# Other addresses for some operands of the matrix products in a two-layer MoE kernel

## The chip, the core and the metric

The kernel runs on one core of a Trainium2 chip. The metric is the time of one execution on the device in microseconds; a lower number is better. Three runs of the kernel before took 1744.85, 1748.18 and 1754.96 us, median 1748.18.

## What is computed

Attention with pooled keys and values (batch 8, 8 heads, 576 positions, 64 per head), then two feed-forward layers on the 4608 tokens of 512 features:

```python
# attention: keys and values averaged over 8 positions
x = attn_out.transpose(0, 2, 1, 3).reshape(B * S, H * D)
# first layer, d_ff = 2048
h = x @ w_in
g = h * np.clip(h + 3.0, 0.0, 6.0) / 6.0
x = g @ w_out
# second layer, d_ff = 1536
g = x @ w_gate
silu = g / (1.0 + np.exp(-g))
out = (silu * (x @ w_val)) @ w_out
```

## The kernel before

All products are done in a 4-byte type in three passes: each operand is split into a high part, rounded to the type, and the low rest (`split`: a copy on ACT and a subtraction on DVE), and high x high, high x low and low x high are summed in PSUM. So products come in threes.

The program has these stages, one after the other on PE:

- Attention, woven into the first up-product `up` (L623): 512 columns of tokens stream past 128x128 weights; in groups of 12 products for one tile of 128 hidden features. The last block of tokens has no attention left beside it: 204 products in a row.
- `down_b` (L891), the down-product of the first layer, for 9 blocks of 512 tokens (`NB`). It uses Strassen's scheme in Winograd's form: 7 products of quarter matrices in place of 8. Each of the 7 (`n`, listed in `DN`) walks through 4 chunks (`NCB`) of hidden features, and a chunk is 12 products of 256 columns. The stationary operand is the weights, `pw`, one tile for each of the 7; the moving operand is the chunk `gb`, split just before. 9 x 7 x 4 x 12 = 3024 products.
- For each of 6 groups of 768 tokens (`NG`): `up2` with 504 products of 384 columns (12 weight blocks, each 7 x 6 products; stationary `wr` from a ring of four buffers, moving `xc`, the split token quarters), then `down2` with 378 products of 256 columns (7 x 3 chunks x 18; stationary `gc`, the split chunk, moving `wr`). Both are issued on L712 (`mm3x`).

The order on each engine is the order in which the code is written; pools decide when a buffer is free again. Weights for `pw` come by `load_pw` from SP's queue, half a tile (1 MB) for each DMA.

What matters here is where operands lie in a partition of SBUF. In this text the **distance** of a product is the address of its moving operand less that of its stationary operand, in bytes, modulo 256. In the built program before it is 0 for all 1728 products of L623, 64 for all 3024 of `down_b`, 0 for all 3024 of `up2` and 64 for all 2268 of `down2`. Tiles with `+ 64` elements of room and a start at element 8 (`ring_tile`, `x_step`) serve to set it. In the attention, the products of L601 to L604 (256 columns at most) have their moving operand 32 above the stationary one.

In `x_step`, `what` names the quarter or sum of quarters: `11`, `T1`, `T2`, `21`, `T4`, `T3`, `22`; the seven products of a block use them in the order P1 (11), P6 (T2), P5 (T1), P2 (21), P4 (T4), P7 (T3), P3 (22). In `split_gc`, `n` counts the seven products of `down2` and `c` their three chunks.

Of the kernel before, what the change touches and what calls it, by code (L numbers as in the profile page):

```python
# [9 lines left out]
F32R = mybir.dt.float32r  # L10
# [8 lines left out]
def f32(ap):  # L19
    return ap.bitcast(F32)  # L20
# [3 lines left out]
def kernel(  # L24
# [27 lines left out]
    nc = tc.nc  # L52
    P = 128
# [31 lines left out]
    half = const.tile([P, 1], F32, name="half")  # L85
    gap_p.tile([P, 16], F32, name="gap")

    BIG = 4096
# [11 lines left out]
    M = 384  # L100
# [5 lines left out]
    NP1 = F1 // 2  # L106
    g_d = [dram.tile([P, 2, 2, NP1, MB], F32, name=f"g{j}") for j in range(NB)]
    s_w1 = dram.tile([P, 7, NP1, 2, 2 * P], F32, name="sw1")
# [90 lines left out]
    B7 = {"11": 0, "T1": 1, "21": 2, "T2": 3, "22": 4, "T3": 5, "T4": 6, "12": 7}  # L199
# [441 lines left out]
    def store_g(j, f, g):  # L641
# [8 lines left out]
    DN = [("P1", "11", "11"), ("P4", "22", "T4"), ("P2", "12", "21"), ("P6", "S2", "T2"),  # L650
          ("P5", "S1", "T1"), ("P7", "S3", "T3"), ("P3", "S4", "22")]
    HALF = 4
    CH = 2
    l2 = {}
    xc, ys, gf, gc, wr = {}, {}, {}, {}, {}

    def load_y(p):
# [5 lines left out]
            nc.sync.dma_start(out=t[:, 2 * r + c], in_=y_d[:, 2 * r:2 * r + 2, t0:t0 + M])  # L663
        ys[p] = t

    def x_step(p, n, lo_eng, sum_eng):

        t = ys[p]
        place = {"11": 0, "T1": 0, "12": 1, "T3": 1, "21": 2, "T4": 2, "22": 3, "T2": 3}
        v = lambda what: t[:, place[what]]  # L670
        what, then = [("11", "T1"), ("22", "T3"), ("T1", "T2"), ("T2", None), ("21", "T4"), ("T4", None), ("T3", None)][n]
        if what == "11":
            x = new_q7("xc")
        else:
            pool = l2["xa" if what in ("T1", "22") else "xt" if what == "T3" else "xb"]
            x = pool.tile([P, 4 * M + 64], F32R, tag="x" + what, name="xc")
        x = xc[p, what] = x[:, 8:8 + 4 * M].rearrange("p (a k n) -> p a k n", a=2, k=2)
        split(x[:, 0], x[:, 1], v(what), lo_eng)
        if then:
            sums_b(sum_eng, v, (then,))  # L680
# [87 lines left out]
    def split_gc(p, n, c, lo_eng):  # L768

        what = DN[n][1]  # L770
        t = gc[p, n, c] = l2["gc"].tile([P, 2, CH, M], F32R, tag="gc", name="gc")
        split(t[:, 0], t[:, 1], gf[p][:, GP[what], CH * c:CH * (c + 1)], lo_eng)

    def sums_g(p, ops, a, b):
# [65 lines left out]
    CB = 2  # L840
# [4 lines left out]
    def load_g(j, slot):  # L845

        if j < NB:
            r, c = divmod(slot, 2)
            t = gq[j, slot] = lb["gq"].tile([P, NP1, MB], F32, tag=f"gq{slot}", name="gq")
            nc.sync.dma_start(out=t, in_=g_d[j][:, r, c])  # L850

    def new_pw(n, t):
        lb["pw", DN[n][2]] = t.rearrange("p (f a n) -> p f a n", f=NP1, a=2)

    def load_pw(n, half):
        what, fs = DN[n][2], slice(NP1 // 2 * half, NP1 // 2 * (half + 1))
        nc.sync.dma_start(
            out=f32(lb["pw", what][:, fs]).rearrange("p f a n -> p (f a n)"),
            in_=s_w1[:, B7[what], fs].rearrange("p f a n -> p (f a n)"),
        )  # L860

    SLOT = {"11": 0, "S1": 0, "12": 1, "S4": 1, "21": 2, "S3": 2, "22": 3, "S2": 3}

# [14 lines left out]
    def down_b(i):  # L878

        j, n = divmod(i, 7)  # L880
        what = DN[n][0]
        place = "P1" if what in ("P6", "P7") else what
        if what == place:
            bb[what] = bank().rearrange("p (d n) -> p d n", d=2)
        ps, w = bb[place], lb["pw", DN[n][2]]
        for c in range(NCB):
            g = gb.pop((i, c))
            for d in range(2):
                for k in range(CB):
                    for m, (wh, gh) in enumerate(((0, 0), (0, 1), (1, 0))):  # L890
                        nc.tensor.matmul(  # L891
                            out=ps[:, d], lhsT=w[:, CB * c + k, wh, P * d:P * (d + 1)], rhs=g[:, gh, k],
                            start=what == place and (c, d, k, m) == (0, 0, 0, 0),
                            stop=(c, k, m) == (NCB - 1, CB - 1, 2), skip_group_check=True,
                        )
# [249 lines left out]
    with tc.manual_schedule():  # L1145
# [64 lines left out]
        for j in range(NB):  # L1210
            for f in range(F1):
                if (j, f) == (NB - 1, 0):
                    attn_ctx.close()
                    for nm in ("px", "gq"):
                        lb[nm] = right_b.enter_context(
                            tc.tile_pool(name=nm, bufs=1, side="right", reuse_waits="tile"))
                    new_pw(0, lb["px"].tile([P, BIG + 8], F32R, tag="px", name="pw")[:, :BIG])
                    new_pw(1, big_x("pw"))
                hp = ps_h.tile([P, N], F32, tag="h", name="h")
                up(hp, wu[f], x_tile(j))  # L1220
                attn_slot(j, 2 * f)
                gate()
                attn_slot(j, 2 * f + 1)
                gated.append((j, f, act1(hp), hp))
                if j == 0:
                    weights.convert()
                else:
                    prep_slot(F1 * (j - 1) + f)
                if j == NB - 1:
                    if f % 4 == 3:  # L1230
                        new_pw(2 + f // 4, big_w("pw"))
                    if f in first_loads:
                        kind, *args = first_loads[f]
                        (load_g if kind == "g" else load_pw)(*args)
                    if f >= F1 - NCB:
                        split_b(0, f - F1 + NCB)
# [106 lines left out]
```

## Time and profile before

| | us |
|---|---|
| median of three runs | 1748.18 |
| the profiled execution | 1749.84 |
| its span, first to last instruction | 1747.8 |
| PE busy in it | 1696.1 |
| DVE busy | 1335.7 |
| ACT busy | 751.9 |
| POOL busy | 640.9 |

The profiled execution is the one from which all rows below come; its span and 2 us around it make up its time. Busy time of PE counts products that overlap only once: a product lasts longer than the distance between the starts of two, since they are pipelined. In the timeline, products of one line that follow each other without a pause are one row, with the first start, the time from there to the last end, and their number.

### The profile page before, as it was taken

The numbers are of one execution on the slowest core, as the hardware profiler recorded it, in microseconds if no ns is written. First come the engines' busy times: TensorE is split into PE (matmuls) and PEld (weight loads), VectorE is DVE, ScalarE is ACT, GpSimd is POOL, SyncE is SP. The second block draws the span as 40 slices with busy tenths as digits, with TensorE's granted clock in tenths as the row PEclk, the third lists the DMA queues.
The fourth block names the chain that finished last, engine by engine and source line by source line (L and its number), as shares of the span: only waits on it lengthen the run. The fifth ranks groups of instructions, "written<-read, shape, count | busy, mean of one in ns | idle before, by whom it ended". The sixth has DMA issues, their size and how long they took to land.

```text
span 1747.8 us, 30757 instructions
## 1 busy us (share of the span) xinstructions
PE 1696.1 (97%) x11116; PEld 1603.2 (92%) x11116; DVE 1335.7 (76%) x2356; ACT 751.9 (43%) x1656; POOL 640.9 (37%) x821
## 2 busy tenths in 40 slices
PE   5889999999999999999999999999999999999999
PEld 4678887878788899999999999999999999999999
DVE  6888898788976678888888668668668668668665
ACT  6665554555544445555554233223224224224222
POOL 6565775766821000000000550550550550560560
PEclk8899999999999999999999999999999999999999
DMA  7766898888767965555555878878878878878776
GB/s 184 180 181 186 244 278 261 238 260 255 227 228 279 415 256 190 194 204 215 212 182 188 289 240 290 296 241 288 295 243 289 293 242 289 297 241 287 265 241 217
DMA packets 237784, 432.48 MB, mean 247 GB/s; under 512 B 87104, under 2 KB 169024, under 8 KB 220480
## 3 DMA queue, kind: packets, MB, share of 16 engines
q1 hardware_dynamic: 236576, 430.25, 74.7%
q8 instruction: 88, 1.44, 0.3%
q14 instruction: 64, 0.52, 0.1%
q10 hardware_dynamic: 1056, 0.26, 0.1%
HBM read 326.11 MB, written 104.33 MB: 246 GB/s over the span
## 4 chain that ended last, share of the span: by engine, by line
PE 86%; DVE 6%; DMA 4%; ACT 2%; issue 1%; POOL 1%; SPq 0%; DVEq 0%; POOLq 0%; ACTq 0%
PE b L712 45%; PE b L891 20%; PE h L623 17%; PE pss L503 1%; DMA q_in<-in_q_dram 1%; DVE g L638 1%; DMA wstg<-in_moe_w_in_dram 1%; PE pst L573 1%; PE pst L577 1%; PE psv L601 0%; DVE vtl L469 0%; DVE mx L513 0%; DVE qT L485 0%; PE psv L602 0%; PE psv L604 0%
## 5 line engine op out<-in xcount | busy, mean ns | idle before, releaser
L712 PE MATMUL b<-xc,wr 128*128 128x384 f32 x3024 | 527.3, 335 | 3.0 <-ACT xc L149 2.4
L712 PEld LDWEIGHTS b<-xc,wr 128*128 128x128 f32 x3024 | 525.5, 188 | 3.6 <-ACT xc L149 2.8
L623 PE MATMUL h<-x,wu 128*128 128x512 f32 x1728 | 430.0, 400 | 5.3 <-DVE g L638 5.2
L759 POOL TENSOR_TENSOR s<-s,c 128x384 f32<-128x384 f32 x144 | 142.5, 1016 | 754.3 <-ACT s L757 754.3
L721 DVE TENSOR_TENSOR c<-c,b 128x384 f32<-128x384 f32 x504 | 265.0, 552 | 175.1 <-PE b L712 151.3
L623 PEld LDWEIGHTS h<-x,wu 128*128 128x128 f32 x1728 | 320.1, 191 | 70.9 <-DVE g L638 6.7
L891 PE MATMUL b<-gb,pw 128*128 128x256 f32 x3024 | 356.8, 279 | 0.7 <-ACT gb L149 0.7
L891 PEld LDWEIGHTS b<-gb,pw 128*128 128x128 f32 x3024 | 356.4, 188 | 1.1 <-ACT gb L149 0.9
L712 PE MATMUL b<-wr,gc 128*128 128x256 f32 x2268 | 268.1, 279 | 0.0
L712 PEld LDWEIGHTS b<-wr,gc 128*128 128x128 f32 x2268 | 267.9, 188 | 0.0
L149 ACT CAST gb<-gq 128x512 fp32r<-128x512 f32 x252 | 155.0, 621 | 158.4 <-PE b L891 133.6
L150 DVE TENSOR_TENSOR gb<-gq,gb 128x512 fp32r<-128x512 f32 x252 | 167.6, 689 | 53.9 <-ACT gb L149 53.2
L766 POOL TENSOR_TENSOR gf<-s,c 128x384 f32<-128x384 f32 x144 | 168.4, 1195 | 66.6 <-DVE c L721 64.3
L149 ACT CAST gc<-gf 128x768 fp32r<-128x768 f32 x126 | 105.6, 838 | 189.0 <-POOL gf L766 101.0
L757 ACT ACTIVATE s<-c 128x384 f32<-128x384 f32 x144 | 73.4, 526 | 198.2 <-DVE c L721 197.0
L150 DVE TENSOR_TENSOR gc<-gf,gc 128x768 fp32r<-128x768 f32 x126 | 134.2, 1094 | 18.0 <-ACT gc L149 16.3
L634 ACT ACTIVATE g<-h,half 128x512 f32<-128x512 f32 x144 | 98.9, 687 | 75.7 <-PE h L623 61.4
L638 DVE SCALAR_TENSOR_TENSOR g<-g,h 128x512 f32<-128x512 f32 x144 | 97.4, 677 | 22.7 <-ACT g L634 22.5
L551 POOL TENSOR_TENSOR e<-e,sm 128x288 f32<-128x288 f32 (+4 forms) x74 | 48.3, 653 | 123.1 <-DVE sm L547 87.4
L729 ACT COPY c<-b 128x384 f32<-128x384 f32 x72 | 34.0, 472 | 128.5 <-PE b L712 128.5
L869 DVE TENSOR_TENSOR gq<-gq 128x1024 f32<-128x1024 f32 x72 | 87.8, 1219 | 0.0
L207 DVE TENSOR_TENSOR gf<-gf 128x768 f32<-128x768 f32 (+1 forms) x66 | 66.9, 1029 | 12.1 <-POOL gf L766 10.9
(101 smaller groups left out, 1657.4 us busy)
## 6 DMA issues: line engine op xcount, KB each, us to landing
wr<-sup SPq DMA_DIRECT2D x72, 1024.0 KB
wr<-sdn SPq DMA_DIRECT2D x84, 768.0 KB
wr<-sup SPq DMA_DIRECT2D x72, 768.0 KB
g<-g SPq DMA_DIRECT2D x144, 256.0 KB
gq<-g SPq DMA_DIRECT2D x36, 1024.0 KB
wstg<-in_moe_w_out_dram SPq DMA_DIRECT2D x56, 256.0 KB
pw<-sw SPq DMA_DIRECT2D x14, 1024.0 KB
sup<-s SPq DMA_DIRECT2D x12, 1024.0 KB
```

The lines of the kernel that those rows point to most:

```text
L149: nc.scalar.copy(out=hi, in_=src)
L150: lo_engine.tensor_tensor(out=lo, in0=src, in1=f32(hi), op=ALU.subtract)
L623: nc.tensor.matmul(out=ps, lhsT=w(kt, wh), rhs=x(kt, xh), start=first and n == 0, stop=last and n == 3 * len(kts) - 1,)
L634: nc.scalar.activation(out=t, in_=ps, func=ACTF.Relu, bias=half, scale=1.0 / 6.0)
L638: nc.vector.scalar_tensor_tensor(out=t, in0=t, scalar=1.0, in1=ps, op0=ALU.min, op1=ALU.mult)
L712: nc.tensor.matmul(out=ps, lhsT=w(wh), rhs=x(xh), start=first and n == 0, stop=last and n == 2)
L721: add = lambda dst, a, b: nc.vector.tensor_tensor(out=dst, in0=a, in1=b, op=ALU.add)
L757: nc.scalar.activation(out=g[q], in_=c[q], func=ACTF.Sigmoid)
L759: nc.gpsimd.tensor_tensor(out=g[q], in0=g[q], in1=c[q], op=ALU.mult)
L766: nc.gpsimd.tensor_tensor(out=gf[p][:, GP[TURN[q]], f], in0=g[q], in1=c[q], op=ALU.mult)
L869: nc.vector.tensor_tensor(out=v(what), in0=v(a), in1=v(b), op=op)
L891: nc.tensor.matmul(out=ps[:, d], lhsT=w[:, CB * c + k, wh, P * d:P * (d + 1)], rhs=g[:, gh, k], start=what == place and (c, d, k, m) == (0 ...
```

## The change

It gives other start addresses to some operand tiles, so that part of the products have another distance. Number, order and size of the products stay, line for line (the lines move by 4 to 11).

| stage | before | after |
|---|---|---|
| `down_b` | 3024 at 64 | in each of 9 blocks: 12 at 0, 12 at 64, 12 at 96, 12 at 0 (the four chunks of n = 0), then 288 at 64 |
| `up2` | 3024 at 0 | in each of 72 weight blocks of 42: 18 at 0 (P1, P6, P5), 6 at 64 (P2), 6 at 0 (P4), 6 at 32 (P7), 6 at 0 (P3) |
| `down2` | 2268 at 64 | in each of 6 groups: 18 at 0, 144 at 64, 18 at 96, 36 at 64, 18 at 0, 144 at 64 |

In all that is 2700 + 1944 products of 256 columns at 64, 432 at 0 and 216 at 96, and of the 384-column products 2160 at 0, 432 at 64 and 432 at 32.

```diff
+    GC_AT = {(0, 0): 16, (3, 0): 56, (4, 0): 16}
+    X_AT = {'21': 24, 'T3': 16}
+
     def x_step(p, n, lo_eng, sum_eng):
...
-        x = xc[p, what] = x[:, 8:8 + 4 * M].rearrange("p (a k n) -> p a k n", a=2, k=2)
+        a = X_AT.get(what, 8)
+        x = xc[p, what] = x[:, a:a + 4 * M].rearrange("p (a k n) -> p a k n", a=2, k=2)
...
     def split_gc(p, n, c, lo_eng):

         what = DN[n][1]
-        t = gc[p, n, c] = l2["gc"].tile([P, 2, CH, M], F32R, tag="gc", name="gc")
+        a = GC_AT.get((n, c), 0)
+        t = l2["gc"].tile([P, 2 * CH * M + 64], F32R, tag="gc", name="gc")[:, a:a + 2 * CH * M]
+        t = gc[p, n, c] = t.rearrange("p (a k n) -> p a k n", a=2, k=CH)
...
+    P1_AT = (16, 1088, 2168, 3216)
+
     def new_pw(n, t):
-        lb["pw", DN[n][2]] = t.rearrange("p (f a n) -> p f a n", f=NP1, a=2)
+        k = BIG // NCB
+        at = P1_AT if n == 0 else [k * c for c in range(NCB)]
+        lb["pw", DN[n][2]] = [t[:, a:a + k].rearrange("p (f a n) -> p f a n", f=CB, a=2) for a in at]

     def load_pw(n, half):
-        what, fs = DN[n][2], slice(NP1 // 2 * half, NP1 // 2 * (half + 1))
-        nc.sync.dma_start(
-            out=f32(lb["pw", what][:, fs]).rearrange("p f a n -> p (f a n)"),
-            in_=s_w1[:, B7[what], fs].rearrange("p f a n -> p (f a n)"),
-        )
+        what = DN[n][2]
+        for c in range(NCB // 2 * half, NCB // 2 * (half + 1)):
+            nc.sync.dma_start(
+                out=f32(lb["pw", what][c]).rearrange("p f a n -> p (f a n)"),
+                in_=s_w1[:, B7[what], CB * c:CB * (c + 1)].rearrange("p f a n -> p (f a n)"),
+            )
...
-                            out=ps[:, d], lhsT=w[:, CB * c + k, wh, P * d:P * (d + 1)], rhs=g[:, gh, k],
+                            out=ps[:, d], lhsT=w[c][:, k, wh, P * d:P * (d + 1)], rhs=g[:, gh, k],
...
-                    new_pw(0, lb["px"].tile([P, BIG + 8], F32R, tag="px", name="pw")[:, :BIG])
+                    new_pw(0, lb["px"].tile([P, 4296], F32R, tag="px", name="pw"))
```

The only instructions that are added are DMAs of SP. This is SP's order at the last of them, at the beginning of `down_b`, before (`g` are the stores of the first layer's gated values, `pw` the weights of `down_b`, `y` its results, `gq` the gated values read back for the next block of tokens):

```order
L642 DMA g_105<-g_7257 256x1x256
L642 DMA g_105<-g_7278 256x1x256
L857 DMA pw<-sw_106 128x2048 x8
L912 DMA y<-o_7496 128x2x256
L850 DMA gq<-g_98 128x2048 x4
```

and the same place after:

```order
L642 DMA g_105<-g_7262 256x1x256
L642 DMA g_105<-g_7284 256x1x256
L868 DMA pw<-sw_106 128x1024 x16
L923 DMA y<-o_7510 128x2x256
L856 DMA gq<-g_98 128x2048 x4
```

The eight DMAs have become sixteen of half the size, in the same place. The first six loads of `pw`, which stand singly between stores of `g`, have become pairs in the same way:

```order
 L283 DMA sup_116<-s_6907 128x1536
-L857 DMA pw<-sw_106 128x2048
+L868 DMA pw<-sw_106 128x1024 x2
 L642 DMA g_105<-g_6954 256x1x256
 L123 DMA wstg<-in_moe_w_val_dram 128x2x256 x2
```

## Rows read from the trace of the kernel before

**Rows 1.** The page: span, busy time of PE and DVE, the chain that ended last.

```profile
span 1747.8 us, 30757 instructions
...
PE 1696.1 (97%) x11116; PEld 1603.2 (92%) x11116; DVE 1335.7 (76%) x2356; ACT 751.9 (43%) x1656; POOL 640.9 (37%) x821
...
PE 86%; DVE 6%; DMA 4%; ACT 2%; issue 1%; POOL 1%; SPq 0%; DVEq 0%; POOLq 0%; ACTq 0%
PE b L712 45%; PE b L891 20%; PE h L623 17%; PE pss L503 1%; DMA q_in<-in_q_dram 1%; DVE g L638 1%; DMA wstg<-in_moe_w_in_dram 1%; PE pst L573 1%; PE pst L577 1%; PE psv L601 0%; DVE vtl L469 0%; DVE mx L513 0%; DVE qT L485 0%; PE psv L602 0%; PE psv L604 0%
```

**Rows 2.** Timeline of PE, stages after the attention: start us, us, what, count, idle before.

```profile
543.78 46.44 PE L623 MATMUL h<-x,wu 128*128 128x512 f32 x204
590.07 17.34 PE L891 MATMUL b<-gb,pw 128*128 128x256 f32 x144
608.09 339.44 PE L891 MATMUL b<-gb,pw 128*128 128x256 f32 x2880 [0.68 <-ACT gb L149]
...
1039.83 44.68 PE L712 MATMUL b<-wr,gc 128*128 128x256 f32 x378
1084.35 87.53 PE L712 MATMUL b<-xc,wr 128*128 128x384 f32 x504
1171.71 44.68 PE L712 MATMUL b<-wr,gc 128*128 128x256 f32 x378
...
1611.87 87.53 PE L712 MATMUL b<-xc,wr 128*128 128x384 f32 x504
1699.23 44.68 PE L712 MATMUL b<-wr,gc 128*128 128x256 f32 x378
```

**Rows 3.** Products by line: count, duration of one in ns (min/median/max), first and last start.

```profile
L623 PE MATMUL h<-x,wu x432: 387/389/497, 479.7 to 589.8; 128*128 128x512 f32 x144
...
L712 PE MATMUL b<-xc,wr x3024: 333/334/525, 947.4 to 1699.1; 128*128 128x384 f32 x189
L712 PE MATMUL b<-wr,gc x2268: 276/279/281, 1039.8 to 1743.6; 128*128 128x256 f32 x189
```

**Rows 4.** Timeline of PE at the end of the attention, trains of L623 and single products.

```profile
514.29 2.90 PE L623 MATMUL h<-x,wu 128*128 128x512 f32 x12
...
540.06 0.28 PE L601 MATMUL psv<-aT,vst 128*128 128x256 f32 x1
540.18 0.28 PE L602 MATMUL psv<-aT,vst 128*128 128x256 f32 x1
540.30 0.28 PE L603 MATMUL psv<-aT,vst 128*128 128x256 f32 x1
540.41 0.28 PE L604 MATMUL psv<-aTt,vtl 96*128 96x256 f32 x1
540.54 2.93 PE L623 MATMUL h<-x,wu 128*128 128x512 f32 x12
543.30 0.28 PE L601 MATMUL psv<-aT,vst 128*128 128x256 f32 x1
543.43 0.28 PE L602 MATMUL psv<-aT,vst 128*128 128x256 f32 x1
543.55 0.28 PE L603 MATMUL psv<-aT,vst 128*128 128x256 f32 x1
543.66 0.28 PE L604 MATMUL psv<-aTt,vtl 96*128 96x256 f32 x1
```

**Rows 5.** The same timeline earlier, attention products of 64 columns.

```profile
479.39 0.28 PE L602 MATMUL psv<-aT,vst 128*128 128x64 f32 x1
479.50 0.28 PE L603 MATMUL psv<-aT,vst 128*128 128x64 f32 x1
479.61 0.28 PE L604 MATMUL psv<-aTt,vtl 96*128 96x64 f32 x1
```

**Rows 6.** Three stretches (`down_b`, `up2`, `down2`): busy us (count) by engine, clock, DMA.

```profile
core 0: us, PE busy (x) PEld busy (x) DVE busy (x) ACT busy (x) POOL busy (x), PEclk, DMA share, GB/s
608.00:947.00 339.00, 338.92 (x2877) 338.95 (x2878) 289.83 (x411) 176.07 (x290) 0.00 (x0) 1.00 0.58 206
1084.35:1171.71 87.36, 87.36 (x506) 87.36 (x505) 55.43 (x95) 21.35 (x41) 47.58 (x46) 1.00 0.82 280
1171.71:1216.23 44.52, 44.52 (x380) 44.52 (x379) 38.62 (x52) 20.06 (x29) 4.26 (x3) 1.00 0.81 268
```

**Rows 7.** Timeline of SP's queue at the beginning of `down_b`.

```profile
596.47 9.39 SPq L857 DMA_DIRECT2D pw<-sw  x8
609.41 0.37 SPq L912 DMA_DIRECT2D y<-o  x1
615.44 11.63 SPq L850 DMA_DIRECT2D gq<-g  x4
```

## The prediction

> **What bounds the kernel now.** I read the page first: busy shares, then the chain that ended last [rows 1]. PE is busy 97% of the span, and three lines of matrix products hold 82% of the chain: L712 45%, L891 20%, L623 17%. No wait of any size stands between them, so from the middle of the kernel on the time is the number of products times the spacing between their starts. That spacing is read from the timeline of PE, where products that follow each other without a pause are one row [rows 2]. A row lasts from the first start to the last end, so I take off one product's own length (medians of 279, 334 and 389 ns for 256, 384 and 512 columns, [rows 3]) and divide by the count less one:
>
> - L623 after the attention, 512 columns, distance 0: (46.44 - 0.389)/203 = 226.85 ns.
> - L712 in `up2`, 384 columns, distance 0: (87.53 - 0.334)/503 = 173.35 ns.
> - L891, 256 columns, distance 64: (339.44 - 0.279)/2879 = 117.81 ns.
> - L712 in `down2`, 256 columns, distance 64: (44.68 - 0.279)/377 = 117.77 ns.
>
> The granted clock is 1.00 in these stretches [rows 6], the upper level, 2.4 GHz, where one column per cycle would be 213.3, 160.0 and 106.7 ns. So each product costs more than its columns: 13.5 and 13.35 ns at distance 0, 11.1 ns at distance 64. This surplus, not waits or other engines, is what the change can touch: 11.1 ns on 5292 products of 256 columns is 59 us, 13.35 ns on 3024 of 384 columns is 40 us.
>
> The surplus isn't one fixed number. In the attention part L623 runs in trains of 12 products. A train of the same count lasts 2.90 us in one place and 2.93 in another [rows 4]: (2.93 - 0.389)/11 = 231.0 ns a product against 226.85 in the long run, 46 ns more in a train; the shorter train has 228.3. So after other products have come between, a run needs some products to settle, and until then each costs some 4 ns more. What went before matters, at least for a while.
>
> **The change part by part.** The number, order and size of products stay. Sum against the profiled execution, 1749.84 us, span 1747.8; the median of the three runs, 1748.18, lies 0.1% below it, and I add the sum to the median.
>
> 1. The long runs, 2700 products in `down_b` and 1944 in `down2` still at distance 64, now led in by 12 or 18 products of 256 columns at distance 0. Is a led-in run faster? The trace of before has this already in another shape: each of the six `down2` stretches follows 504 products at distance 0, and `down_b` follows 204 of them. All six `down2` rows read 44.68 us [rows 2], and the run of L891 that starts afresh after an idle time of 0.68 us has the same spacing, 117.81 [rows 2]. So the long run at distance 64 shows one spacing, from three different beginnings. I take 0 for this term. It is the one that would matter: 1 ns here is 4.6 us.
> 2. 432 products of 256 columns go to distance 0. None of that size and distance is in the trace. By the rows at distance 0 the surplus is 13.4 ns whatever the columns, so 120.1 ns, 2.3 more than now: +1.0 us. Other end: the products of L601 to L604 (256 columns, distance 32) start (540.41 - 540.06)/3 = 0.117 us apart [rows 4]: -0.3 us.
> 3. 216 products of 256 columns go to distance 96. Nearest rows: L601 to L604 again, from 0.117 on the mean of three to 0.13 for the one pair at 543.30 [rows 4]. I take 120 ns, the mean at 543.30: +0.5 us; ends -0.2 and +2.6.
> 4. 432 products of `up2` go to distance 64. With the surplus of the rows at 64, 160.0 + 11.1 = 171.1 against 173.35: -1.0 us; the other end is no gain, 0.
> 5. 432 products of `up2` go to distance 32. Surplus from the same 120 ns at 256 columns: 13.3, as now, so 0; ends -1.3 (from 117) and +1.8 (4.1 ns more, as in an unsettled train).
> 6. The pieces break the `up2` run. 72 times (12 weight blocks in 6 groups) two pieces of 6 end, and the products at distance 0 behind them may have to settle. One unsettled train costs 46 ns [rows 4]. I take half of that, once per block: 72 x 0.023 = +1.7 us; ends 0 and two whole trains, 72 x 0.092 = +6.6.
> 7. `load_pw` sends 28 DMAs of half the size in place of 14. The last eight of before, now sixteen, fill the tiles of the fourth to seventh product group; they are issued in a row from 596.47 on, 1.17 us each [rows 7]. The fourth group starts at 608.09 after an idle time of 0.68 us [rows 2], and each group lasts 48 x 0.1178 = 5.65 us. If a half-size DMA also takes 1.17 us to issue, the four of a group are out by 601.2, 605.8, 610.5 and 615.2, at least 7 us before the groups begin; the bytes are the same. Queued behind them on SP are a store of `y` and the loads of `gq` that begin at 615.44 [rows 7], of which the first may start up to 9.4 us later; they are for the next token block, 40 us away. Cost 0; without this cover up to 9.4 us, or back to -0.7 if the idle time at 608 goes.
> 8. The splits on ACT and DVE write the same number of elements at other addresses: 0. Their cover is the 14% of DVE that is free in `down_b`, 289.83 of 339 us being busy [rows 6].
>
> Sum: +1.0 + 0.5 - 1.0 + 0 + 1.7 = +2.2 us, ends -2.8 and +12.0. Forecast 1748.2 + 2.2 = **1750.4 us**, its own range 1745 to 1760.
>
> Whether addresses matter at all can be doubted. The spacings of L623 differ by 4 ns between trains of the same instruction [rows 4], so something beyond the columns acts on them. The Trainium skill, page SBUF — State Buffer, section "Who interferes with whom", says that only the port pair which VectorE and GpSimd share causes contention, so where a tile lies would not matter to TensorE. By that rule every term above is 0 and the time 1748.2. The trace neither shows nor excludes it, and it is the third rival below. The same skill, page TensorE: Matmul & The Clock Gate, section "Back-to-back issue gap", gives N/2.4 + 2.5 ns for a warm product, an estimate of 109.2 at 256 columns; no row here is that low, and by it the long runs could give back 8.6 ns each.
>
> **The rivals.**
>
> *The lead-in does work: the run at 64 has a second, faster rhythm that only a lead-in of 256 columns reaches.* For it: the surplus depends on history in L623, and the surplus in question is large. Against it: three kinds of beginning, one spacing. Its floor is in the rows: products of 64 columns in the attention part, whose streaming is short, still start 0.11 us apart [rows 5], so what paces them must be the load of weights; a 256-column product can hardly be below 112. Half way between 112 and 117.8 is 114.9: 2.9 x 4644 = -13.5 us, 1734.7 us; at the floor -27 us, 1721. DVE would follow: 86% busy in `down_b` becomes 88%. It counts as faster from 8.7/4644 = 1.9 ns a product, 115.9.
>
> *The pieces unsettle `up2` for good.* If the 2160 products left at distance 0 never settle between pieces of 6 and stretches of 24, each pays the 4.1 ns of an unsettled train [rows 4]: 2160 x 4.1 = +8.9 us in place of the 1.7, with terms 2 to 5 together +0.5: +9.4 us, 1757.6. It ends slower from 8.7 us, that is if 4 ns a product stay on nearly all of them. For it: settling took up to a whole train of 12. Against it: a train of 2.90 us is settled after a third of its products, by the same 4 ns.
>
> *Distance is no cause at all:* what set 117.8 and 173.35 is the columns alone and history is that of the queue. Then nothing moves: 1748.2.
>
> **How the numbers follow.** What a measurement can tell from no change is about 0.5%, 8.7 us. Forecast (long runs unchanged, small terms) 0.38; no cause at all 0.08; faster rhythm 0.38, of which 0.03 stays within 0.5%; unsettled `up2` 0.16. Within 0.5%: 0.38 + 0.08 + 0.03, less 0.03 for the forecast's upper end, 0.46; faster 0.35, slower 0.19. Range for 8 in 10: down to 1728, which leaves out the deeper third of the faster case (about 0.13), up to 1760 (leaves out about 0.06).
>
> **What would show it.** In the timeline of PE after: rows of `down2` near 44.7 us and of L902 near 117.8 ns say that term 1 is 0; 43.6 us or less, the faster rhythm. Rows of `up2` of 504 products at 87.3 to 87.8 us say that terms 4 to 6 are small; 89 us, the unsettled rival. All rows unchanged to 0.02 us say that distance is no cause. The forecast is wrong if the long runs leave 117.8 ns in either direction.

## The result, and the profile after

The changed kernel takes 1734.93 us (median of 5 runs, 1729.84 to 1737.34) beside 1749.34 us of the kernel before (5 runs, 1744.85 to 1754.96) on the same chip: a ratio of 0.991, 95% interval 0.988 to 0.994. That is faster by 0.9%. The forecast was 1750.4 us, no change; the time is the one worked out for the first rival, 1734.7 us.

The page of the kernel after, the lines that answer to [rows 1]:

```profile
span 1735.4 us, 30785 instructions
...
PE 1685.9 (97%) x11116; PEld 1591.3 (92%) x11116; DVE 1334.3 (77%) x2356; ACT 752.0 (43%) x1656; POOL 642.4 (37%) x821
...
PE 80%; DMA 9%; DVE 7%; SPq 2%; issue 1%; ACT 1%; POOL 0%; DVEq 0%; ACTq 0%; POOLq 0%
```

PE still works 97% of the span, with the same 11116 products, but 10.2 us less. Its share of the chain of waits is down from 86%, because ahead of `down_b` the chain now goes back through DMAs of `gq` and `pw` (to 603 us) and no longer through the long run of L623. Where the time went, the timeline of PE tells (start us, us, what, count, idle before), as in [rows 2]:

```profile
545.27 46.44 PE L623 MATMUL h<-x,wu 128*128 128x512 f32 x204
591.55 348.51 PE L902 MATMUL b<-gb,pw 128*128 128x256 f32 x3024
...
944.76 89.19 PE L716 MATMUL b<-xc,wr 128*128 128x384 f32 x497 [0.30 <-DVE xc L150]
1033.80 43.35 PE L716 MATMUL b<-wr,gc 128*128 128x256 f32 x378
1076.98 87.77 PE L716 MATMUL b<-xc,wr 128*128 128x384 f32 x504
1164.59 43.35 PE L716 MATMUL b<-wr,gc 128*128 128x256 f32 x378
```

Every later row of `up2` and `down2` reads 87.77 and 43.35, too. The stretch of `down2` was 44.68 us and is 43.35; that of `up2` was 87.53 and is 87.77. Measured from the first start of a stage to the first start of the next:

| | before, us | after, us | difference |
|---|---|---|---|
| L623, the long run | 46.29 | 46.28 | 0.0 |
| `down_b` | 357.29 | 348.35 | -8.9 |
| `up2`, six stretches | 529.27 | 531.92 | +2.65 |
| `down2`, six stretches | 267.28 | 259.29 | -8.0 |

That is -14.3 us. The attention ahead of it, which the change doesn't touch, was 1.5 us longer in this execution. Its length differs from one execution to the next: in the kernels of this study `down_b` starts between 585.9 and 595.1 us. So below the rows of the stages decide, and the total time only where there are several runs.

The durations of one product of L902 (min/median/max in ns, as in [rows 3]), and three stretches that answer to [rows 6] (busy us and count by engine, granted clock, DMA):

```profile
L902 PE MATMUL b<-gb,pw x3024: 276/276/388, 591.6 to 939.8; 128*128 128x256 f32 x189
```

```profile
core 0: us, PE busy (x) PEld busy (x) DVE busy (x) ACT busy (x) POOL busy (x), PEclk, DMA share, GB/s
600.00:939.00 339.00, 338.85 (x2946) 338.12 (x2945) 295.83 (x421) 180.50 (x298) 0.00 (x0) 1.00 0.61 218
1076.98:1164.59 87.61, 87.61 (x507) 87.61 (x505) 55.45 (x95) 21.36 (x41) 47.59 (x46) 1.00 0.82 283
1164.59:1207.78 43.19, 43.19 (x380) 43.19 (x379) 38.44 (x52) 20.06 (x29) 4.25 (x3) 1.00 0.81 270
```

In 339 us of `down_b` PE starts 2946 products where it started 2877, at the same granted clock, 1.00. DVE follows: 295.83 us busy of 339 in place of 289.83, 87%.

What a single product costs now is read from the starts of the products in the trace, start to start, by size and distance. Late starts behind a wait are left out; they make some 1.1 us of `down_b` in either kernel.

| columns, distance | before, ns | after, ns |
|---|---|---|
| 256 at 64, `down2` | 117.8 | 113.4 |
| 256 at 64, `down_b` | 117.8 | 114.2 |
| 256 at 0 | - | 119.8 |
| 256 at 96 | - | 119.3 |
| 384 at 0 | 173.35 | 174.15 |
| 384 at 64 | - | 172.5 |
| 384 at 32 | - | 173.5 |

The run at 64 has a second, faster rhythm: 113.33 ns from one start to the next, held without a fault through whole stretches. `down_b` has a higher mean because in two of its nine blocks it falls back to 117.8 ns where PE had to wait for `gb`. The windows of L902 over single blocks of 336 products show it (the first, third and fifth of the nine; a block all at 113.3 behind its lead-ins takes 38.32 us):

```profile
591.55:631.25 39.70, 39.64 (x336) 39.44 (x336) 1.00 1.03 413
...
669.80:708.12 38.32, 38.32 (x338) 38.32 (x337) 1.00 0.63 201
...
746.44:786.40 39.96, 39.87 (x339) 39.67 (x337) 1.00 0.55 200
```

The blocks that start at 591.55 and 746.44 have waits in them: 0.06 and 0.09 us idle by the line (39.70 less 39.64 and so on), and 0.33 and 0.36 us of late starts, since the product before still covers part of the wait. Both are far less than the 1.4 and 1.6 us by which these blocks are longer: the rest is the slower rhythm behind the wait, until the next lead-in. A piece at 96 doesn't end the faster rhythm: in `down2` the 36 products behind it are at 113.3 again.

SP's queue, as in [rows 7]:

```profile
598.68 18.36 SPq L868 DMA_DIRECT2D pw<-sw  x16
```

Sixteen DMAs of half the size take 18.36 us to issue, 1.15 us each, and PE waits for none of them.

### The profile page after: what moved, and what is told of

It reads as the page before. It is cut to its first block, busy times and chain, and to the rows that moved or that the text cites. A ratio compares the mean times of both kernels' runs of the same rounds, so it can differ in the third digit from the quotient of the medians.

```text
span 1735.4 us, 30785 instructions
## 1 busy us (share of the span) xinstructions
PE 1685.9 (97%) x11116; PEld 1591.3 (92%) x11116; DVE 1334.3 (77%) x2356; ACT 752.0 (43%) x1656; POOL 642.4 (37%) x821
## 4 chain that ended last, share of the span: by engine, by line
PE 80%; DMA 9%; DVE 7%; SPq 2%; issue 1%; ACT 1%; POOL 0%; DVEq 0%; ACTq 0%; POOLq 0%
PE b L716 45%; PE b L902 18%; PE h L623 13%; DMA q_in<-in_q_dram 2%; DMA g<-g 1%; DMA gq<-g 1%; PE pss L503 1%; SPq L384 1%; DVE g L638 1%; DMA wstg<-in_moe_w_in_dram 1%; DMA sup<-s 1%; DMA qv<-in_q_dram 1%; DVE qT L485 1%; DMA pw<-sw 1%; DVE vtl L469 1%
## 5 line engine op out<-in xcount | busy, mean ns | idle before, releaser
L623 PE MATMUL h<-x,wu 128*128 128x512 f32 x1728 | 432.3, 402 | 5.5 <-DVE g L638 5.5
L623 PEld LDWEIGHTS h<-x,wu 128*128 128x128 f32 x1728 | 322.0, 192 | 71.2 <-DVE g L638 6.6
L902 PE MATMUL b<-gb,pw 128*128 128x256 f32 x3024 | 348.4, 277 | 0.1
L902 PEld LDWEIGHTS b<-gb,pw 128*128 128x128 f32 x3024 | 347.6, 188 | 1.0 <-DVE gb L150 0.9
L716 PE MATMUL b<-wr,gc 128*128 128x256 f32 x2268 | 260.1, 277 | 0.0
L716 PEld LDWEIGHTS b<-wr,gc 128*128 128x128 f32 x2268 | 259.9, 188 | 0.0
```

What stands on the lines that cost most here:

```text
L623: nc.tensor.matmul(out=ps, lhsT=w(kt, wh), rhs=x(kt, xh), start=first and n == 0, stop=last and n == 3 * len(kts) - 1,)
L716: nc.tensor.matmul(out=ps, lhsT=w(wh), rhs=x(xh), start=first and n == 0, stop=last and n == 2)
L902: nc.tensor.matmul(out=ps[:, d], lhsT=w[c][:, k, wh, P * d:P * (d + 1)], rhs=g[:, gh, k], start=what == place and (c, d, k, m) == (0, 0, 0 ...
```

## The experiments

The theory after the result: products of 256 columns at distance 0, right in front of a run at 64, bring the run into the rhythm of 113.3 ns, and it stays there until PE waits. The rivals: it is the pieces at other distances (an interruption of any kind) that do it; it is the changed `up2` in front of `down2`; any other distance would serve; or it is not the distance but the place of one operand. All edits are against the changed kernel, in the tables that it brought, if not said otherwise.

**The pieces of `up2` alone.** `down_b` and `down2` are at 64 throughout.

```diff
-    GC_AT = {(0, 0): 16, (3, 0): 56, (4, 0): 16}
+    GC_AT = {}
...
-    P1_AT = (16, 1088, 2168, 3216)
+    P1_AT = (0, 1024, 2048, 3072)
```

> Only the pieces of up2 are at 64 and 32; both down stages as before, all at 64. Theory A: down2 rows 44.7 us, up2 rows 87.8 us, time 1.5 us over the kernel before, not to be told from it. Rival (the run at 64 takes its rhythm from how up2 ends): down2 rows 42.9 us with no lead-in at all, down_b unchanged at 117.8 ns, time about 8 us below.

One run, 1751.0 us. The timeline of PE, two stretches:

```profile
1039.50 44.68 PE L716 MATMUL b<-wr,gc 128*128 128x256 f32 x378
1084.01 87.77 PE L716 MATMUL b<-xc,wr 128*128 128x384 f32 x504
```

`down2` takes what it took before, behind the changed `up2` as behind the old one, and `up2` is 0.24 us a stretch longer. So the pieces of `up2` bring nothing and cost 1.4 us.

**Everything but the lead-ins at distance 0.** The pieces at 96 and those of `up2` stay.

```diff
-    GC_AT = {(0, 0): 16, (3, 0): 56, (4, 0): 16}
+    GC_AT = {(3, 0): 56}
...
-    P1_AT = (16, 1088, 2168, 3216)
+    P1_AT = (0, 1024, 2104, 3136)
```

> All pieces at 32, 64 and 96 of the changed kernel stay, the products at distance 0 of 256 columns go back to 64. Theory A: without lead-in the runs at 64 stay at 117.8 ns, the down2 rows at 44.7 us, time about 2 us over the kernel before. Rival (a piece at 96, or the unsettled end of up2, does it as well): the runs behind the pieces at 113.3 ns, down2 43.2 us, time some 15 us below.

One run, 1747.3 us.

```profile
585.89 356.95 PE L902 MATMUL b<-gb,pw 128*128 128x256 f32 x3024
...
1035.42 44.72 PE L716 MATMUL b<-wr,gc 128*128 128x256 f32 x378
```

3024 products in 356.95 us are (356.95 - 0.28)/3023 = 118.0 ns each, in one row: all of the gain in `down_b` is gone, and that in `down2`, too. A piece at 96 in the middle of a run, and what it interrupts, does nothing.

**The lead-ins at distance 0 alone.** One of 12 in each block of `down_b`, one of 18 in each stretch of `down2`.

```diff
-    GC_AT = {(0, 0): 16, (3, 0): 56, (4, 0): 16}
-    X_AT = {'21': 24, 'T3': 16}
+    GC_AT = {(0, 0): 16}
+    X_AT = {}
...
-    P1_AT = (16, 1088, 2168, 3216)
+    P1_AT = (16, 1088, 2112, 3136)
```

> Only the lead-ins stay: 12 products at distance 0 at the head of each token block in down_b and 18 at the head of each down2; everything else has the distance of the kernel before. Theory A (256-column products at distance 0 alone bring the run at 64 into the faster rhythm): down2 rows stay at about 43.0 us, the long runs at 113.3 ns, up2 rows return to 87.5 us; against the changed kernel 216 products at 0 and 216 at 96 fewer (216 x 6.6 + 216 x 5.9 = 2.7 us) and 1.5 us of up2 back: some 19.5 us under the kernel before, ratio about 0.989. Theory B (the pieces at 32, 64 and 96 are needed to put the lead-in into step): down2 rows 44.7 us, 117.8 ns, no change of time, ratio 1.00.

1727.9 us (median of 5 runs, 1726.06 to 1730.42), before 1747.54 on this chip: a ratio of 0.988, interval 0.986 to 0.990. That is faster than the kernel before. Beside the changed kernel (0.991, 0.988 to 0.994) the intervals of the ratios overlap, and the rows decide. The timeline of PE:

```profile
588.01 203.56 PE L902 MATMUL b<-gb,pw 128*128 128x256 f32 x1777
791.88 144.33 PE L902 MATMUL b<-gb,pw 128*128 128x256 f32 x1247 [0.31 <-DVE gb L150]
...
1158.70 43.11 PE L716 MATMUL b<-wr,gc 128*128 128x256 f32 x378
1201.65 87.53 PE L716 MATMUL b<-xc,wr 128*128 128x384 f32 x504
```

`up2` is back at 87.53. `down2` takes 43.11 us: (43.11 - 0.276)/377 = 113.6 ns a product with the lead-in, which is 18 products at some 119.3 ns and 359 at (42.83 - 18 x 0.1193)/359 = 113.3. So the lead-in alone does all of it, and the other pieces of the change cost: 0.24 us in each of twelve stretches, and 38.32 - 38.16 = 0.16 in each block of `down_b`, together some 4.3 us.

The blocks of `down_b`, by windows of L902 (us, PE busy and count, weight loads, clock, DMA):

```profile
588.01:627.70 39.69, 39.69 (x336) 39.50 (x336) 1.00 1.03 412
627.70:665.86 38.16, 38.16 (x339) 38.16 (x337) 1.00 0.53 189
...
742.18:780.34 38.16, 38.16 (x339) 38.16 (x337) 1.00 0.56 203
780.34:820.14 39.80, 39.49 (x338) 39.29 (x337) 1.00 0.55 198
820.14:859.74 39.60, 39.60 (x338) 39.60 (x337) 1.00 0.54 195
859.74:897.89 38.15, 38.15 (x338) 38.15 (x337) 1.00 0.57 203
```

A block in the fast rhythm takes 38.16 us (12 at 120 and 324 at 113.33 are 38.16), one in the slow rhythm 39.60 (324 at 117.77). The first block, 39.69, shows no idle time, but by the single starts one product of its second group began 271 ns after the one before it, and the block is slow from there on. The block at 780.34 holds the wait of 0.31 us for `gb`, and is slow from there on, too. The next, at 820.14, has no wait at all and is slow to its end: its lead-in, begun from the slow rhythm, didn't take. In the single starts its 12 products run 121, 120, 124, 117, 118 and again, where a lead-in that takes settles at 120. The lead-in of the block after that takes again. Nor does every wait end the rhythm. In the kernel of whole stretches at other distances (below; its `down_b` is the same as here) a wait at the same place as the one of 0.31 us left the rhythm as it was, and the same 1247 products took 2.5 us less:

```profile
794.01 141.84 PE L902 MATMUL b<-gb,pw 128*128 128x256 f32 x1247 [0.17 <-DVE gb L150]
```

By the single starts, 21 waits fell into the faster rhythm of `down_b` in the ten kernels of this study that have lead-ins at 0 there, and 19 of them ended it. So the rhythm is a state: most waits end it, and a lead-in of 12 brings it back in most cases, but neither in all. What tells these cases apart isn't shown.

**The same lead-ins at distance 96.**

```diff
-    GC_AT = {(0, 0): 16, (3, 0): 56, (4, 0): 16}
-    X_AT = {'21': 24, 'T3': 16}
+    GC_AT = {(0, 0): 56}
+    X_AT = {}
...
-    P1_AT = (16, 1088, 2168, 3216)
+    P1_AT = (56, 1088, 2112, 3136)
```

> As the kernel with lead-ins only, but the lead-ins are at distance 96 in place of 0. Theory A in its narrow form (it must be distance 0): the runs at 64 at 117.8 ns, time about that of before. In its wide form (any 256-column products at another distance move the start): 113.3 ns behind them and some 19 us below.

One run, 1745.58 us, with `down2` at 44.7 again:

```profile
1035.00 44.72 PE L716 MATMUL b<-wr,gc 128*128 128x256 f32 x378
```

**A lead-in at each other distance**, in front of `down2` alone. `p` is the group; the six values give 32, 224, 192, 160, 128 and 0. The kernel of the lead-ins alone is the base here and in what follows.

```diff
-        a = GC_AT.get((n, c), 0)
+        a = (8, 24, 32, 40, 48, 16)[p] if (n, c) == (0, 0) else 0
```

> Lead-ins at distance 0 alone, as in the first experiment, but in down2 the 18 products of the lead-in stand at distances 32, 224, 192, 160, 128 and (last stretch) 0, the rest at 64. Theory (only distance 0 does it): the last stretch 43.1 us, the first five 44.7 us, time 1727.9 + 5 x 1.6 = 1735.9 us. Rival (any change of distance of the right size does it): more than one stretch at 43.1 us; each that does takes 1.6 us off.

One run, 1736.88 us. The first, the fifth and the last stretch:

```profile
1028.10 44.67 PE L716 MATMUL b<-wr,gc 128*128 128x256 f32 x378
...
1555.63 44.69 PE L716 MATMUL b<-wr,gc 128*128 128x256 f32 x378
...
1687.53 43.11 PE L716 MATMUL b<-wr,gc 128*128 128x256 f32 x378
```

The other three read 44.67 to 44.69. Of the seven distances of a lead-in that were run (96 in the kernel above), 0 alone does it.

**Whole stretches at other distances**, without and with a lead-in at 0. In the first kernel `down2` stands at 32, 224, 192, 160, 128 and 96 throughout, `up2` at 32, 64, 96, 128, 160 and 192; in the second 18 (or, in `up2`, 42) products at 0 go ahead of each stretch, and the rest of `down2` stands at 32, 96, 128, 160, 192 and 224.

```diff
-        a = X_AT.get(what, 8)
+        a = (16, 24, 32, 40, 48, 56)[p]
...
-        a = GC_AT.get((n, c), 0)
+        a = (8, 24, 32, 40, 48, 56)[p]
```

> down_b as with lead-ins at distance 0 alone. No lead-in in down2; the six down2 stretches (378 products of 256 columns) stand whole at distances 32, 224, 192, 160, 128 and 96, the six up2 stretches (504 of 384 columns) whole at 32, 64, 96, 128, 160 and 192. Theory (a distance has spacings of its own and only products of 256 columns at distance 0 bring the run at 64 into the faster one): the stretches differ by distance: 96 near 120.0 ns (45.5 us a stretch), the others between 113.3 and 120 (43.1 to 45.6 us), up2 at 32 and 64 between 172.5 and 173.5 ns (87.1 to 87.6 us). Rival (only distance 0 is special and all others are like 64): down2 44.7 us and up2 87.1 us in every stretch. Rival (what comes before decides, not the distance): down2 stretches follow up2 at other distances here and could be at 113.3 ns from the first product. Time 1733 to 1743 us.

One run, 1745.5 us, above the range that was expected. The timeline of PE, five of the stretches:

```profile
1029.44 45.52 PE L716 MATMUL b<-wr,gc 128*128 128x256 f32 x378
1074.79 87.53 PE L716 MATMUL b<-xc,wr 128*128 128x384 f32 x504
...
1206.89 89.20 PE L716 MATMUL b<-xc,wr 128*128 128x384 f32 x504
1295.93 44.68 PE L716 MATMUL b<-wr,gc 128*128 128x256 f32 x378
...
1605.74 88.19 PE L716 MATMUL b<-xc,wr 128*128 128x384 f32 x504
```

The second, against the kernel of the lead-ins alone:

```diff
-        a = GC_AT.get((n, c), 0)
+        a = 16 if (n, c) == (0, 0) else (8, 56, 48, 40, 32, 24)[p]
...
-            t = ring_tile()
+            t = ring_tile(8 if u == (0, 0) else (0, 56, 48, 40, 32, 24)[sent[0] // len(stream)])
```

> Lead-ins at distance 0 in down_b, down2 and up2 (18 products of 256 columns in front of down2, the first 42 of 384 columns in front of up2); what follows stands at distances 32, 96, 128, 160, 192 and 224 in the six down2 stretches and 32, 64, 96, 128, 160 and 192 in the six up2 stretches. Theory (the faster rhythm belongs to 256 columns at distance 64 behind distance 0): down2 44.5 to 45.5 us in every stretch, as without a lead-in, up2 87.5 to 89.2 us; time 1740 to 1746 us. Rival (a lead-in at distance 0 brings other distances, or products of 384 columns, into a faster rhythm too): down2 43.2 us in some stretches, or up2 84.2 us (504 x 166.7 ns) in some.

One run, 1747.75 us, above the expected range as well:

```profile
1032.11 44.31 PE L716 MATMUL b<-wr,gc 128*128 128x256 f32 x378
1076.26 87.53 PE L716 MATMUL b<-xc,wr 128*128 128x384 f32 x504
...
1607.70 89.07 PE L716 MATMUL b<-xc,wr 128*128 128x384 f32 x504
```

The spacings that follow from all the rows of both ((length - 0.276)/377 or (length - 0.334)/503; behind a lead-in, that of the rest):

| distance | 256 columns, whole stretch | behind 18 at 0 | 384 columns, whole stretch | behind 42 at 0 |
|---|---|---|---|---|
| 32 | 120.0 | 116.7 | | |
| 64 | 117.8 | **113.3** | 173.35 | 173.35 |
| 96 | 120.0 | 120.0 | 176.7 | 176.7 |
| 128 | 118.7 | 118.7 | 176.0 | 176.0 |
| 160 | 117.4 | 117.3 | 173.35 | 173.35 |
| 192 | 117.8 | 117.8 | 174.7 | 176.7 |
| 224 | 118.3 | 118.3 | | |

So the spacing differs by distance, over 2.6 ns with 256 columns and 3.4 with 384, and some distances have two, by what came before: 64 and 32 with 256 columns. (The 44.31 us at 32 lies below the 44.5 to 45.5 that the theory gave.) With 384 columns 192 has two as well, but there the two kernels don't tell why: in the first the moving operand was placed otherwise, in the second the stationary one. (The rows of `up2` at 32 hold the start of the stage and are left out.) Without a lead-in no stretch came to 113.3. Nothing beats 64 behind 0; and no stretch of `up2` is below the 173.35 ns that it has anyway.

**A lead-in for `up2`.** Its first 42 products at 32, 224, 192, 160, 128 and 96, the others at 0.

```diff
-            t = ring_tile()
+            t = ring_tile((0, 16, 24, 32, 40, 48)[sent[0] // len(stream)] if u == (0, 0) else 8)
```

> Lead-ins at distance 0 alone in down_b and down2, and the first 42 products of 384 columns of each up2 stretch at distances 32, 224, 192, 160, 128 and 96, the other 462 at 0. Theory (the second rhythm is one of products of 256 columns at 64): all six up2 stretches 87.5 us, the pieces within 0.2 us of that, time 1727 to 1729 us. Rival (up2 too has a faster rhythm, 4 ns lower, that some lead-in reaches): at least one stretch at 85.5 us or less (504 x 169.2 ns), 2 us off for each.

One run, 1730.41 us. The rows of the five undisturbed stretches read 87.52 to 87.66, within 0.13 of those without a lead-in, so `up2` found no second rhythm. The span is 1728.5 us beside 1727.4 of the kernel of the lead-ins alone; the difference is `down_b`, where two lead-ins of 12 didn't take this time. Products of 512 columns weren't tried.

**The lead-in made by the moving operand.** So far every lead-in at distance 0 came from the place of the stationary operand: `gc` (or `pw`) lies 64 bytes further on than in the run. Here the weight block, the moving one, lies 192 bytes further on, which modulo 256 is 64 bytes lower, and `gc` stays. In the first kernel the order of the products breaks the lead-in up: 21 at 0, then threes at 64 and at 0 by turns. In the second it is unbroken, 18 at 0.

```diff
-            t = ring_tile()
+            t = ring_tile(56 if (n, h) == (0, 0) else 8)
```

> As the first experiment, but down2's lead-in at distance 0 is made by the place of the weight block (the moving operand), not by that of the split of gc (the stationary one): 21 at 0, then threes at 64 and 0 by turns, then 345 at 64 unbroken. Theory (the distance between both addresses decides): down2 at 113.3 ns after the threes, 43.3 us or less a stretch, time 1728 to 1730 us. Rival (the place of the stationary operand itself decides): 117.8 ns, 44.7 us a stretch, time 1737.5 us.

One run, 1746.36 us, in an execution with a long attention part (`down_b` starts at 595.09). All six rows of `down2` read 44.75 us.

The second kernel's edit, in `load_dn` (`t` is the whole ring tile, and the block comes with two DMAs):

```diff
+                nc.sync.dma_start(out=f32(t[:, 56:56 + 1024]), in_=src[:, :1024])
+                nc.sync.dma_start(out=f32(t[:, 1096:1096 + 512]), in_=src[:, 1024:1536])
+                at = [56, 56 + 512, 1096]
```

> down2's lead-in of 18 products at distance 0 is made by the place of the first two weight blocks (moving operand), unbroken, with the split of gc where it was in the kernel before; else as the first experiment. Theory (the distance decides, and the lead-in must end settled): down2 43.1 us in every stretch, time 1728 to 1730 us. Rival (the place of the stationary operand decides, so moving the other one does nothing): 44.7 us, time 1737 us.

One run, 1739.3 us:

```profile
1160.78 44.72 PE L723 MATMUL b<-wr,gc 128*128 128x256 f32 x378
```

All six stretches are at 44.72. The lead-in itself is the same by the single starts: 18 products that settle at 120 ns. Yet the run behind it is slow. So the theory that the distance decides falls, as far as it says that the distance is enough.

**Which step of which operand.** Six kinds of lead-in in one kernel, one for each stretch of `down2`. `GC_LEAD` places the stationary operand of the lead-in and `W_LEAD` the first two weight blocks, which come by DMAs of their own in all six.

```diff
+    GC_LEAD, W_LEAD = (16, 32, 48, 16, 8, 32), (24, 24, 40, 8, 0, 24)
...
+        a = GC_LEAD[p] if (n, c) == (0, 0) else (0, 0, 0, 0, 0, 16)[p]
```

> As the first experiment, but the first 18 products of the six down2 stretches differ in where their operands lie against the products behind them, in bytes, stationary and moving: +64 and +64 (distance 64 as in the run), +128 and +64 (distance 0), +192 and +128 (0), +64 and 0 (0, as in the first experiment), +32 and -32 (0), and in the last stretch +64 and 0 with all of its operands 64 bytes further on (0). Each stretch is 43.1 us when the run behind is at 113.3 ns and 44.7 us when it is at 117.8. Theory J (the step of the stationary operand by 64 bytes at the switch decides): 43.1 in the first, fourth and sixth, 44.7 in the others; 1737.5 - 3 x 1.6 = 1732.7 us. Theory Z (a lead-in at distance 0 whose stationary operand lies elsewhere, by whatever step): 43.1 in all but the first, 1729.5 us. Theory JZ (both, distance 0 and the step of 64): 43.1 in the fourth and the sixth alone, 1734.3 us. If the place in the memory counts in itself, the sixth is at 44.7.

One run, 1738.38 us, 4 us above the sum of the theory that fits the rows; 1.4 of them are in `down_b`, 349.5 us beside the 348.0 of the kernel of the lead-ins alone. The first, fourth, fifth and sixth stretch (the second reads 44.71, the third 44.72):

```profile
1031.11 44.67 PE L725 MATMUL b<-wr,gc 128*128 128x256 f32 x378
...
1426.82 43.11 PE L725 MATMUL b<-wr,gc 128*128 128x256 f32 x378
...
1557.13 44.71 PE L725 MATMUL b<-wr,gc 128*128 128x256 f32 x378
...
1689.05 43.12 PE L725 MATMUL b<-wr,gc 128*128 128x256 f32 x378
```

The fourth and the sixth are fast, the others slow, as the theory that wants both says. All kinds of lead-in that were run in front of a run at 64 in `down2` (steps in bytes, modulo 256), by where the operands of the lead-in lie against those of the run:

| distance of the lead-in | stationary | moving | run at 64 behind |
|---|---|---|---|
| 0 | +64 | 0 | 113.3 |
| 0, all operands 64 further on | +64 | 0 | 113.3 |
| 0 | 0 | -64 | 117.8 |
| 0 | +32 | -32 | 117.8 |
| 0 | +128 | +64 | 117.8 |
| 0 | +192 | +128 | 117.8 |
| 64 | +64 | +64 | 117.8 |
| 32, 96, 128, 160, 192, 224 | other | 0 | 117.8 |

So of all these, the lead-in works that is at distance 0 and at whose end the stationary operand steps by 64 bytes while the moving one stays in its place. At distance 0 the two steps hang together (the stationary one is the moving one and 64 more), so these runs can't say which of them decides, and other steps weren't tried. Where both lie in memory didn't count in the one other place that was tried. How few products a lead-in needs wasn't tried either.

**The lead-in of `down_b` behind the waits.** It stands at the third product in place of the first: `P1_AT` serves n = 2, and the tiles of n = 0, 1 and 2 change places.

```diff
-        at = P1_AT if n == 0 else [k * c for c in range(NCB)]
+        at = P1_AT if n == 2 else [k * c for c in range(NCB)]
```

> As the first experiment, but the lead-in of 12 in down_b stands in front of the third product group of a block in place of the first, behind the places where most waits for gb fall. Theory (a wait throws the run back to 117.8 ns until the next lead-in): the first two groups of block 0 (96 products) stay at 117.8, the later ones are at 113.3, and what a wait in groups 0 to 2 costs ends with the lead-in; 1 to 3 us less than the first experiment, 1725 to 1727 us. Rival (the losses after a wait lie elsewhere, or new waits come for the weights whose tiles changed places): 1728 us or more.

1730.05 us (median of 4 runs, 1728.27 to 1732.1), a ratio of 0.989, interval 0.988 to 0.991. `down_b` in the profile, the first and the last of three rows:

```profile
588.30 159.84 PE L902 MATMUL b<-gb,pw 128*128 128x256 f32 x1393
...
792.91 141.90 PE L902 MATMUL b<-gb,pw 128*128 128x256 f32 x1247 [0.34 <-DVE gb L150]
```

From 588.30 to 934.64, the start of `up2`, `down_b` takes 346.3 us, 1.7 less than the 348.0 with the lead-in in front, though two gaps lie in it. That is the size that was expected, and by the single starts the first two groups of block 0 are at 117.8 and all nine lead-ins took, as the theory says. The median missed the 1725 to 1727 us that was expected and lies where the rival put it, above 1728. The totals don't tell the two kernels apart: they ran on different chips, and the intervals of the ratios overlap. It stays open which is faster.

## Why the prediction was wrong

**Term 1, the long runs, is the step that failed.** It was put at 0; it measures 2700 x (117.8 - 114.2) = 9.7 us in `down_b` and 1944 x (117.8 - 113.4) = 8.6 us in `down2`, 18.3 us in all. The term rested on "three different beginnings, one spacing" [rows 2]: 504 products at distance 0, 204 products at distance 0, an idle time. But the first two have 384 and 512 columns, and none of the three has a stationary operand that steps by 64 bytes under a moving operand that stays. The rows were read rightly; what they showed was that these beginnings do nothing, and not that no beginning does. Nothing in the trace of before came near the beginning that the change makes, so the term should have been bounded by the rival's price instead of being set to 0.

**The other terms, measured:**

| term | forecast, us | measured, us |
|---|---|---|
| 2: 432 of 256 columns at 0 | +1.0 | 432 x 2.0 ns = +0.9 |
| 3: 216 at 96 | +0.5 | 216 x 1.5 = +0.3 |
| 4: 432 of `up2` at 64 | -1.0 | 432 x -0.85 = -0.4 |
| 5: 432 of `up2` at 32 | 0 | 432 x 0.15 = +0.1 |
| 6: pieces unsettle `up2` | +1.7 | 2160 x 0.8 = +1.7 |
| sum | +2.2 | +2.6 |

Term 2's rule, the surplus of distance 0 whatever the columns, held to 0.3 ns (120.1 forecast, 119.8). Term 6 shows in the single starts: behind the pieces some products take 175 to 185 ns, and then the run is back at 173.3. The rival with an `up2` that never settles would have given rows of 89 us; they are 87.77. Term 4 is the one with the wrong working: a stretch of `up2` wholly at 64 has 173.35 ns, as at 0, so the surplus doesn't go over from 256 to 384 columns there.

**Terms 7 and 8** were right: no product waits for `pw`, the DMAs are as long as forecast (1.15 us, 1.17 assumed), and DVE's busy time stays (1334.3 us beside 1335.7).

**What the sum missed besides** is 1.2 us in the first stretch of `up2`, 89.19 us here. At its beginning PE waits for `xc`, in both kernels, which "no wait of any size" in the prediction passed over. The windows behind that wait, of the kernel after and then of the kernel before (us, PE busy and count, granted clock, DMA):

```profile
944.76:946.00 1.24, 1.24 (x4) 0.50 0.68 243
946.00:948.00 2.00, 2.00 (x8) 0.50 0.44 154
948.00:950.00 2.00, 2.00 (x8) 0.50 0.00 0
```

```profile
954.00:956.00 2.00, 2.00 (x8) 0.53 0.14 49
956.00:958.00 2.00, 2.00 (x13) 1.00 0.17 33
```

After pauses of 3 us in all the granted clock falls to 0.50, the lower of the two levels, 1.2 GHz, and products are 320 ns apart: for some 5.5 us after the change, for some 3.5 before. All kernels of this study have these pauses. Behind them eleven have 7 to 16 products at 320 ns, and three, the kernel of the lead-ins alone among them, have none and a clock of 1.00. No run ties the length to the addresses; what sets it isn't shown.

**The rivals.** The first, a faster rhythm that only a lead-in of 256 columns reaches, is what happened, at 1734.7 us forecast and 1734.9 measured. Its floor of 112 from the products of 64 columns [rows 5] and its half-way value of 114.9 had the measured 113.33 between them. That forecast and measurement agree to 0.2 us is luck, since two sizes compensate: the gain in the runs was greater, 18.3 us in place of 13.5, and the small terms and the first `up2` took some 4 us back. Its condition was too wide: not any lead-in of 256 columns does it. That the load of weights is what sets the floor no run shows. The last rival, no cause at all, fell with it, and with it the reading of the rule that the Trainium skill gives on the page SBUF — State Buffer, section "Who interferes with whom", as one that would let places not matter to TensorE: products of one size differ by up to 6.7 ns (113.3 to 120.0) by the places of their operands. The other figure quoted there, an estimate of 109.2 ns by the Trainium skill's page TensorE: Matmul & The Clock Gate, section "Back-to-back issue gap", is that section's formula for a product by itself and not for a stream of weight loads and products. No steady run here reached it; 113.33 is the lowest.

**The range** (1728 to 1760) holds the time; the forecast and its chances stood on the wrong side, with 0.35 for faster.

## What to carry to other kernels

The spacing of TensorE's products can be a state: the same products at the same addresses ran at 113.3 or 117.8 ns for hundreds of products, by what stood in front of them and, in most cases, whether the engine had waited. So beginnings of another size or with other operands stepping don't speak for a new one, and a term that a trace can't show is to be bounded, not set to 0. Where a tuned kernel is bound by the spacing, a lead-in of 12 to 18 products at distance 0, made by the place of the stationary operand alone and put behind the places where the engine waits, is a cheap trial, and the pieces that don't carry it are to be left out.

## What the runs showed of the hardware

- Products of 256 columns in the 4-byte type start 113.3 to 120.0 ns apart by the distance of their operands and by what came before, those of 384 columns 173.3 to 176.7, all at a granted clock of 1.00.
- Distance 64 with 256 columns has two steady rhythms, 113.33 and 117.8 ns. Of 21 waits of PE that fell into the first one, 19 ended it, the shortest with a start 271 ns behind the one before; one with a start 445 ns behind didn't. It comes back in most cases behind a lead-in of 12, and in all behind one of 18 (none of which began from the slower rhythm), at distance 0 whose stationary operand lies 64 bytes further on while the moving one stays.
- The same lead-in made by the moving operand, equally settled at 120 ns, leaves the run at 117.8. Why isn't shown: the trace tells when weight loads and products start and not what their reads of the memory do in between.
